# Windowed attention and a gated feed-forward block: scores of six groups in 64-key blocks on quarters of the matmul array

## The chip, the core and the metric

The kernel runs on one core of a Trainium2 chip. A core has a matmul engine (TensorE; PE for its matmuls and PEld for its weight loads in the profile), a vector engine (VectorE, DVE), a scalar engine (ScalarE, ACT), GpSimd (POOL) and SyncE (SP), which here only issues DMAs. Matmuls read SBUF and write PSUM, which has 8 banks; a bank holds 512 fp32 columns on each of 128 partitions. The metric is the time of one execution on the device in microseconds (us). The matmul array has 128 x 128 cells and can be divided into tiles; the profile writes a tile's rows and columns as 64\*128 or 64\*64.

## The reference

```python
scores = scale * np.matmul(q, k.transpose(0, 1, 3, 2))
is_sink = pos[None, :] < n_sink                 # 4
rel = pos[:, None] - pos[None, :]
in_window = (rel >= 0) & (rel < window)         # 128
scores = np.where(is_sink | in_window, scores, -1e9)
a = np.exp(scores - max); a = a / sum(a)
x = np.matmul(a, v)                             # tokens x (heads * 64)
g = x @ w_gate
out = (g * sigmoid(g) * (x @ w_val)) @ w_out
```

There are 4 batches, 8 heads, 768 positions and 64 elements a head; the feed-forward block has 3072 tokens, width 512 and inner width 1536. A query sees itself, the 127 keys before it and the first four keys of its batch.

## The kernel before, in words

The order of all instructions is written by hand. Attention runs in 12 groups of 256 queries, three to a batch (`b, c = divmod(g, 3)`); the feed-forward block runs in eight token blocks of 256 or 512. The two are interleaved on the same engines: `weave` goes through the feed-forward units (`gate`: gate and value projections of 128 inner columns, L414; `down`: output projection of 128 tokens, L499) and puts attention steps between their matmuls, at the units that `slots` and `pair` list (L686 to L719). Each engine runs its own instructions strictly in that order. Work for DVE that belongs to a step is put in the list `later` and issued at the next `flush`.

For a group, `step_S` (L271) makes the scores, transposed (keys on partitions, queries along the columns), for two pairs of heads at a time. The two heads of a pair lie on the upper and the lower 64 partitions of `kTs` and `qTs` and run as two row tiles of 64 x 128. Per head there are 512 columns: four blocks of 128 keys by 128 queries. For the query tile `j` (0 or 1) of 128 queries these are the keys of the tile before it (columns 256j) and its own keys (columns 256j + 128). ScalarE takes the exponential (L293) into `e`, and DVE multiplies two heads by a 0/1 mask (L298). About half of each block is masked away, since the window is a diagonal band. `step_K` (L302) makes the scores of the four sink keys for c > 0, and `step_sinks` (L322) multiplies them by the sink values. It opens four PSUM banks, one for each query tile and half of the heads, with one matmul each. `step_PV` (L332) then adds, for a query tile and four heads, two matmuls a head: `e` of the key tile before and of the own key tile, each times the values with a column of ones (65 columns, L349). The sum of exponentials comes out in column 65; DVE divides (L357, L363), and `step_X` (L369) turns the result for the feed-forward block, by a DMA transpose on SP's queue for all but the first three groups.

`step_sinks` is called at the start of the first `step_PV` of a group (query tile 0, heads 0 to 3). `PVs(g)` lists the four value steps with the head half as the outer loop, so the first two read heads 0 to 3.

Inputs come through GpSimd's DMA queue: `load_nat` (L104; four DMAs for a group's keys and queries), `load_v` (L116; two DMAs, 128 positions each, into a tile `va` of its own per group, whose ones DVE writes). Keys and queries of groups 4 to 11 are turned by `xbar` (L247) on SP's queue, and `load_nat` of the next group waits for that, since it has one buffer. `behind` and `turned` (L530 to L538) make GpSimd wait for a transposed tile, so that later loads don't start sooner.

The first groups have their own steps: group 0 `pair_T`, `pair_S` (L569 to L602), group 1 `step_T` (L214), where four transposes by matmul write every fourth column of a bank from quarters of 64 x 64. `pair_T` writes every second column (L575) from tiles of 128 x 64.

Of the kernel before, what the change touches and what calls it, by code (L numbers as in the profile page):

```python
# [7 lines left out]
FP32 = mybir.dt.float32  # L8
BF16 = mybir.dt.bfloat16
AF = mybir.ActivationFunctionType  # L10
ALU = mybir.AluOpType
# [3 lines left out]
def kernel(  # L15
# [12 lines left out]
    nc = tc.nc  # L28
    P = 128
    B, H, S, D = q.shape  # L30
# [9 lines left out]
    GC = S // 256  # L40
    NG = B * GC
    SIZES = [256, 256, 256, 512, 512, 512, 512, 256]
    assert sum(SIZES) == NTOK and NG == 12
    OFF = [sum(SIZES[:i]) for i in range(len(SIZES))]
    PEX = (0, 1, 2)

    VS = 72
    FCH = [2] * 6
# [2 lines left out]
    scale = 1.0 / float(D) ** 0.5  # L51
# [7 lines left out]
    const = pool("const", 1)  # L59
# [3 lines left out]
    vpool = pool("vpool", 1)  # L63
    kqtp = pool("kqtp", 2)
    epool = pool("epool", 2)
# [12 lines left out]
    def bank(shape, dtype, name):  # L78
        return psum.tile(shape, dtype, tag="b", name=name)
# [24 lines left out]
    def load_nat(g):  # L104
# [8 lines left out]
                    src[b, :, t0:t0 + P].rearrange("h p d -> p h d"))  # L113
        nats[g] = x

    def load_v(g):  # L116
        b, c = divmod(g, GC)
        va = vpool.tile([P, 2, H, VS], BF16, tag=f"va{g}", name="va")
        nc.vector.memset(va[:, :, :, D:D + 1], 1.0)
        for j in range(2):  # L120
            t0 = c * 256 + j * P
            nc.gpsimd.dma_start(  # L122
                va[:, j, :, 0:D], v[b, :, t0:t0 + P].rearrange("h p d -> p h d"))
        vas[g] = va
# [19 lines left out]
    ident = const.tile([P, P], BF16)  # L144
    mask = const.tile([P, 2, 256], BF16)
    mask0 = const.tile([P, 2, 256], BF16)
    diag_h = const.tile([P, 4], BF16)
    vcf = const.tile([P, 1, D + 1], FP32)
    vcl = const.tile([P, B - 1, D + 1], FP32)
# [28 lines left out]
    def load_sinks(t, b0, b1):  # L178
        for h in range(H):
            r = 32 * (h // 4) + NS * (h % 4)  # L180
            nc.sync.dma_start(
                t[r:r + NS, :, 0:D], v[b0:b1, h, 0:NS].rearrange("b s d -> s b d"))
# [18 lines left out]
    kTs, qTs, es_t, e_t, xns, xTs = {}, {}, {}, {}, {}, {}  # L201
    later = []
# [66 lines left out]
        vsbs.append(vsb)  # L269

    def step_S(g, p2, pps=(0, 1)):  # L271
        b, c = divmod(g, GC)
        if g not in e_t:
            e_t[g] = epool.tile([P, H, 512], BF16, tag="e", name="e")
        q0 = c * 256
        parts = [(q0, q0, 256, P), (q0 + P, q0 + P, P, 3 * P)]
        if c > 0:
            parts.insert(0, (q0 - P, q0, P, 0))
        lo = 0 if c > 0 else P
        pss = {2 * pp + h: bank([P, 512], FP32, "s") for pp in pps for h in range(2)}  # L280
        for pp in pps:
            p = 2 * p2 + pp
            for kk, qq, n, col in parts:
                for h in range(2):
                    r = slice(h * D, (h + 1) * D)
                    nc.tensor.matmul(  # L286
                        pss[2 * pp + h][:, col:col + n], kTs[b][r, p, kk:kk + P],
                        qTs[b][r, p, qq:qq + n], start=True, stop=True)
        m = (mask if c > 0 else mask0).rearrange("q (o a) x -> q o (a x)", o=1)
        for pp in pps:  # L290
            h0 = 4 * p2 + 2 * pp
            for h in range(2):
                nc.scalar.activation(  # L293
                    e_t[g][:, h0 + h, lo:512], pss[2 * pp + h][:, lo:512],
                    AF.Exp, scale=scale)

            def dve(e=e_t[g][:, h0:h0 + 2, lo:512]):
                nc.vector.tensor_tensor(  # L298
                    e, e, m[:, :, lo:512].broadcast_to([P, 2, 512 - lo]), op=ALU.mult)
            later.append(dve)  # L300

    def step_K(g):  # L302
# [17 lines left out]
    pos = {}  # L320

    def step_sinks(g):  # L322

        b, c = divmod(g, GC)
        for j in range(2):
            for hh in range(2):
                r = slice(32 * (2 * j + hh), 32 * (2 * j + hh + 1))
                pos[j, hh] = bank([P, 4, D + 1], FP32, "o")
                nc.tensor.matmul(pos[j, hh], es_t[g][r], vsbs[b][r], start=True,  # L329
                                 stop=False, skip_group_check=True)  # L330

    def step_PV(g, j, hh, norm="v"):  # L332
        b, c = divmod(g, GC)
        t = 2 * c + j
        if hh == 0:
            xns[g, j] = xnp.tile([P, DM], BF16, tag="xn", name="xn")
        if c > 0 and j == hh == 0:
            step_sinks(g)
        po = pos.pop((j, hh)) if c > 0 else bank([P, 4, D + 1], FP32, "o")
        mms = []  # L340
        for hq in range(4):
            h = 4 * hh + hq
            if t > 0:
                vp = vas[g][:, 0, h, 0:D + 1] if j else vas[g - 1][:, 1, h, 0:D + 1]
                mms.append((po[:, hq], e_t[g][:, h, 256 * j:256 * j + P], vp))
            mms.append((po[:, hq], e_t[g][:, h, 256 * j + P:256 * (j + 1)],
                        vas[g][:, j, h, 0:D + 1]))
        for i, (o, l, r) in enumerate(mms):
            nc.tensor.matmul(o, l, r, start=(c == 0 and i == 0),  # L349
                             stop=(i == len(mms) - 1),  # L350
                             skip_group_check=True)
# [21 lines left out]
    def step_X(g, j, evict="v"):  # L373
# [6 lines left out]
        elif tb > 1 and off == 0:  # L380
            xTs[tb] = dense(xtp.tile([P, DMC * 512], BF16, tag="xT", name="xT"),
                            DMC, SIZES[tb])
            if tb == 3:
                for i in range(2):
                    xTs[tb, i] = xTs[tb][:, :, 256 * i:256 * (i + 1)]
        if g not in PEX:
            def sp():
# [254 lines left out]
    nc.gpsimd.memset(vcl, 0.0)  # L642
    nc.gpsimd.memset(vcl[:, :, D:D + 1], 1.0)
    load_sinks(vcl, 1, B)

    step_T(1, 0, 0, "a")
    step_T(1, 0, 1, "a")
# [107 lines left out]
```

## Time and profile before

| | us |
|---|---|
| median of 3 runs | 238.09 |
| lowest and highest | 237.35, 238.37 |
| the profiled execution | 238.22 |
| its span, first to last instruction | 236.4 |
| PE busy | 228.7 |
| DVE, ACT, POOL busy | 157.5, 113.0, 75.3 |

In the profile a line such as `L349 PE MATMUL o<-va,e 128*128 128x65 bf16 x352 | 17.2, 194 | 0.1` gives the line of the kernel, the engine, the output and the inputs, the tile of the array, the shape of the moving operand, how many there were, the time in which at least one of them ran, the mean duration of one in ns, and the idle time of the engine in front of them. Matmuls overlap in time, so a mean duration of 194 ns does not say how often one starts. Lines that begin with a time are from the order in time: the start, the time covered by the merged group, the engine and the operation; consecutive instructions of one kind are merged into one line, and a few matmul records are missing from a trace. L numbers are lines of the kernel before.

### The profile page before, as it was taken

What the parts mean: (1) busy time and instruction counts of PE and PEld (TensorE: products, weight loads), DVE (VectorE), ACT (ScalarE), POOL (GpSimd) and SP (SyncE); (2) the same over time, 40 slices, a digit from 0 to 9 for tenths busy, and PEclk for the clock granted to TensorE, in tenths of its full rate; (3) what the DMA queues carried; (4) which work ended last, traced back from release to release, by engine and by line L of the source; (5) the groups of instructions that cost most, each with busy time, mean ns of one, the idle gap of its engine ahead of it and who ended that gap; (6) DMA issues with size and microseconds to landing.
All of it is one profiled execution on the core that took longest, in us unless ns stands there. A gap on an engine that the chain in (4) does not pass through costs nothing.

```text
span 236.4 us, 4873 instructions
## 1 busy us (share of the span) xinstructions
PE 228.7 (97%) x1867; PEld 127.7 (54%) x1893; DVE 157.5 (67%) x333; ACT 113.0 (48%) x230; POOL 75.3 (32%) x102
## 2 busy tenths in 40 slices
PE   8979999999999999999999999999999999999994
PEld 5659645795555644544445444444444445488443
DVE  4898888768650988960888980698970598877000
ACT  4784485467453836412836522655622663333221
POOL 8996875723501409204435350080000000000000
PEclk9999999999999999999999999999999999999999
DMA  7999999995998949997979996599314100200132
GB/s 137 156 191 176 182 199 205 159 145 79 153 225 168 134 72 76 129 134 172 144 114 136 132 140 168 133 87 116 67 24 143 58 3 0 44 3 1 47 132 90
DMA packets 108743, 27.62 MB, mean 117 GB/s; under 512 B 95792, under 2 KB 105776, under 8 KB 108720
## 3 DMA queue, kind: packets, MB, share of 16 engines
q0 software_dynamic: 76640, 13.90, 79.2%
q1 hardware_dynamic: 30672, 11.58, 25.2%
q10 hardware_dynamic: 1408, 1.84, 2.8%
q8 instruction: 15, 0.25, 0.4%
q14 instruction: 8, 0.07, 0.1%
HBM read 28.34 MB, written 6.29 MB: 147 GB/s over the span
## 4 chain that ended last, share of the span: by engine, by line
PE 89%; POOL 3%; DMA 3%; issue 1%; ACT 1%; DVE 1%; POOLq 0%; DVEq 0%; ACTq 0%
PE pv L414 26%; PE pd L499 26%; PE pg L414 26%; PE o L349 4%; PE s L286 4%; DMA wg<-in_moe_w_gate_dram 3%; POOL va L122 1%; POOL rows L100 1%; PE o L329 1%; PE pn L239 1%; POOL x L186 1%; ACT th L434 1%; PE pk L314 1%; PE px L393 0%; DVE u L442 0%
## 5 line engine op out<-in xcount | busy, mean ns | idle before, releaser
L442 DVE SCALAR_TENSOR_TENSOR u<-th,pg 128x512 bf16<-128x512 f32 x72 | 49.2, 683 | 39.4 <-ACT th L434 39.4
L414 PE MATMUL pg<-xT,wg 128*128 128x512 bf16 (+1 forms) x353 | 73.4, 336 | 1.9 <-DMA wg<-in_moe_w_gate_dram 1.2
L434 ACT ACTIVATE th<-pg 128x512 f32<-128x512 f32 x72 | 43.4, 603 | 63.1 <-PE pg L414 57.2
L414 PE MATMUL pv<-xT,wv 128*128 128x512 bf16 (+1 forms) x349 | 72.9, 336 | 0.6 <-ACT e L293 0.2
L499 PE MATMUL pd<-wo,ht 128*128 128x512 bf16 (+2 forms) x292 | 64.5, 371 | 0.5 <-issue 0.2
L414 PEld LDWEIGHTS <-wg 128*128 128x128 bf16 x360 | 35.0, 98 | 29.1 <-DMA wg<-in_moe_w_gate_dram 1.5
L453 DVE TENSOR_TENSOR ht<-u,pv 128x512 bf16<-128x512 bf16 x62 | 42.7, 688 | 9.4 <-PE pv L414 2.5
L293 ACT ACTIVATE e<-s 128x512 bf16<-128x512 f32 (+1 forms) x88 | 42.9, 583 | 3.7 <-PE s L286 3.6
L499 PEld LDWEIGHTS <-ht 128*128 128x128 bf16 x300 | 27.9, 98 | 30.3 <-issue 0.3
L414 PEld LDWEIGHTS <-wv 128*128 128x128 bf16 x360 | 32.1, 98 | 20.3 <-issue 1.7
L504 ACT ACTIVATE ot<-pd 128x512 f32<-128x512 f32 (+1 forms) x24 | 14.3, 596 | 46.7 <-PE pd L499 42.7
L111 POOL DMA_DIRECT2D nat<-in_k_dram x20 | 17.7, 890 | 39.5 <-DMA qT<-nat 35.8
L298 DVE TENSOR_TENSOR e<-e,mask 128x1024 bf16<-128x1024 bf16 (+1 forms) x44 | 27.1, 654 | 3.7 <-ACT e L293 3.7
L122 POOL DMA_DIRECT2D va<-in_v_dram x24 | 21.4, 917 | 4.7 <-DMA wo<-in_moe_w_out_dram 2.5
L363 DVE TENSOR_TENSOR xn<-o,rcp 128x256 bf16<-128x256 f32 x45 | 19.1, 424 | 1.5
L349 PEld LDWEIGHTS <-e 128*128 128x128 bf16 x352 | 15.2, 98 | 7.9 <-issue 0.2
L111 POOL DMA_DIRECT2D nat<-in_q_dram x20 | 17.7, 900 | 1.1 <-DMA wg<-in_moe_w_gate_dram 0.5
L349 PE MATMUL o<-va,e 128*128 128x65 bf16 x352 | 17.2, 194 | 0.1
L286 PE MATMUL s<-qT,kT 64*128 64x128 bf16 (+1 forms) x240 | 13.1, 238 | 0.0
L286 PEld LDWEIGHTS <-kT 64*128 64x128 bf16 x240 | 7.7, 94 | 7.4 <-issue 6.4
L506 DVE TENSOR_SCALAR ot<-pd 128x128 f32<-128x128 f32 x1 | 0.3, 292 | 14.3 <-PE pd L499 14.3
L357 DVE RECIPROCAL rcp<-o 128x4 f32<-128x4 f32 x48 | 8.3, 175 | 1.4 <-PE o L349 1.3
(74 smaller groups left out, 91.5 us busy)
## 6 DMA issues: line engine op xcount, KB each, us to landing
out_dram<-ot SPq DMA_DIRECT2D x17, 256.0 KB
va<-in_v_dram POOLq DMA_DIRECT2D x24, 128.0 KB, 6.2
nat<-in_k_dram POOLq DMA_DIRECT2D x20, 128.0 KB, 4.1
nat<-in_q_dram POOLq DMA_DIRECT2D x20, 128.0 KB, 5.5
wg<-in_moe_w_gate_dram POOLq DMA_DIRECT2D x6, 256.0 KB, 7.9
wv<-in_moe_w_val_dram POOLq DMA_DIRECT2D x6, 256.0 KB, 8.2
wo<-in_moe_w_out_dram POOLq DMA_DIRECT2D x4, 384.0 KB, 11.1
out_dram<-ot ACTq DMA_DIRECT2D x6, 256.0 KB
```

The source lines that it names most:

```text
L111: nc.gpsimd.dma_start(x[:, i, j].rearrange("p (h d) -> p h d", d=D), src[b, :, t0:t0 + P].rearrange("h p d -> p h d"))
L122: nc.gpsimd.dma_start(va[:, j, :, 0:D], v[b, :, t0:t0 + P].rearrange("h p d -> p h d"))
L286: nc.tensor.matmul(pss[2 * pp + h][:, col:col + n], kTs[b][r, p, kk:kk + P], qTs[b][r, p, qq:qq + n], start=True, stop=True)
L293: nc.scalar.activation(e_t[g][:, h0 + h, lo:512], pss[2 * pp + h][:, lo:512], AF.Exp, scale=scale)
L298: nc.vector.tensor_tensor(e, e, m[:, :, lo:512].broadcast_to([P, 2, 512 - lo]), op=ALU.mult)
L349: nc.tensor.matmul(o, l, r, start=(c == 0 and i == 0), stop=(i == len(mms) - 1), skip_group_check=True)
L363: nc.vector.tensor_tensor(xn, po[:, :, 0:D], rcp.broadcast_to([P, 4, D]), op=ALU.mult)
L414: nc.tensor.matmul(ps[:, i * n:(i + 1) * n], ws[fi][:, c, fo * P:(fo + 1) * P], xTs[tb][:, c], start=(c == 0), stop=(c == DMC - 1))
L434: nc.scalar.activation(th, pg, AF.Tanh, scale=0.5)
L442: nc.vector.scalar_tensor_tensor(u, th, 1.0, pg, op0=ALU.add, op1=ALU.mult)
L453: nc.vector.tensor_tensor(hts[tb][:, f:f + 512 // SIZES[tb]].rearrange("p a n -> p (a n)"), u, pv, op=ALU.mult)
L499: nc.tensor.matmul(po, hts[tb][:, f, ts * P:(ts + 1) * P], wos[f // n][:, f % n, lo:hi], start=(f == 0), stop=(f == DFC - 1))
```

## The change

The six groups `QG` = 4, 5, 7, 8, 10 and 11 (the second and third of batches 1 to 3) are computed in blocks of 64 keys.

- Scores (`step_Sq`): per head 384 columns instead of 512. The four 64-key blocks of the band go to quarters of the array: the head picks the upper or lower rows, the key block the lower or upper half of the columns. A pair of heads takes three runs of four matmuls (192, 128 and 64 columns). The exponential and the mask work on 384 columns. The mask `maskq` is built once on GpSimd, behind the loads of the first four groups, from pieces of `mask`.
- Values: the batch's values lie in a tile `vm` of six blocks of 128 positions that are shifted by 64 against the query tiles (`load_vm`: four DMAs for c = 1, two for c = 2, of which two bring 64 positions only; ones by GpSimd). `step_PV` has one matmul a head: the 128 keys from 64 before the query tile's start to 64 after it. What is left of the band are, per query tile and head, two corners of 64 keys by 64 queries. `step_sinks` does these on two diagonal quarters of the array, two at a time, for all eight heads and both query tiles: 32 matmuls of 65 columns, ahead of the first dense one.

PE has 480 instructions more (3788 and 4268 in all); GpSimd has 14 more, six of them DMAs.

```diff
+    QG = [g for g in range(4, NG) if g % GC]
...
+    def load_vm(g):
+        b, c = divmod(g, GC)
+        if b not in vms:
+            vms[b] = vpool.tile([P, 6, H, VS], BF16, tag=f"vm{b}", name="vm")
+            nc.gpsimd.memset(vms[b][:, :, :, D:D + 1], 1.0)
+        def part(t, hs, p0, p1, t0):
+            nc.gpsimd.dma_start(
+                vms[b][p0:p1, t - 1, hs, 0:D],
+                v[b, hs, t0:t0 + p1 - p0].rearrange("h p d -> p h d"))
+        for t in ((1, 2, 3, 4), (5, 6))[c - 1]:
+            p0, p1 = 64 * (t == 1), P - 64 * (t == 6)
+            part(t, slice(0, H), p0, p1, P * t - 64 + p0)
+
     def load_v(g):
+        if g in QG:
+            return load_vm(g)
...
     def step_S(g, p2, pps=(0, 1)):
+        if g in QG:
+            return step_Sq(g, p2, pps)
...
+    def step_Sq(g, p2, pps=(0, 1)):
...
+        q0 = c * 256
+        runs = (((q0, q0, 192, 0), (q0 + 64, q0 + 64, 192, 192)),
+                ((q0 + 128, q0 + 128, 128, 256), (q0 - 64, q0, 128, 0)),
+                ((q0 - 128, q0, 64, 192), (q0 + 192, q0 + 192, 64, 128)))
+        pss = {2 * pp + h: bank([P, 384], FP32, "s") for pp in pps for h in range(2)}
+        for pp in pps:
+            p = 2 * p2 + pp
+            for run in runs:
+                for odd, (kk, qq, n, col) in enumerate(run):
+                    part = slice(64 * (1 ^ odd), 64 * ((1 ^ odd) + 1))
+                    for h in range(2):
+                        r = slice(h * D, (h + 1) * D)
+                        nc.tensor.matmul(
+                            pss[2 * pp + h][part, col:col + n], kTs[b][r, p, kk:kk + 64],
+                            qTs[b][r, p, qq:qq + n], start=True, stop=True,
+                            skip_group_check=True)
...
     def step_sinks(g):
...
+        if g not in QG:
+            return
+        for j in range(2):
+            col, t = (192, 128)[j], 2 * c + j
+            for hq in range(4):
+                for hb in range(2):
+                    for odd in range(2):
+                        h = 4 * hb + hq
+                        r = slice(64 * (1 ^ odd), 64 * ((1 ^ odd) + 1))
+                        nc.tensor.matmul(
+                            pos[j, hb][64 * odd:64 * (odd + 1), hq],
+                            e_t[g][r, h, col:col + 64],
+                            vms[b][r, t + (0 if odd else -2), h, 0:D + 1],
+                            start=False, stop=False, skip_group_check=True)
...
     def step_PV(g, j, hh, norm="v"):
...
+            if g in QG:
+                mms.append((po[:, hq], e_t[g][:, h, 256 * j:256 * j + P],
+                            vms[b][:, t - 1, h, 0:D + 1]))
+                continue
...
     load_sinks(vcl, 1, B)
+    build_maskq()
```

More of the change, by code (lines that the diff above doesn't have):

```diff
@@ L114, in load_nat @@
         nats[g] = x
+    vms = {}
+    def load_vm(g):
[10 more added lines that the diff above has]
+            part(t, slice(0, H), p0, p1, P * t - 64 + p0)
     def load_v(g):
+        if g in QG:
+            return load_vm(g)
         b, c = divmod(g, GC)
@@ L146 @@
     mask0 = const.tile([P, 2, 256], BF16)
+    maskq = const.tile([P, 6, 64], BF16)
     diag_h = const.tile([P, 4], BF16)
@@ L300, in step_S, with build_maskq, dve @@
             later.append(dve)
+    def build_maskq():
+        nc.gpsimd.memset(maskq, 1.0)
+        if True:
+            for odd in range(2):
+                r = slice(64 * (1 ^ odd), 64 * ((1 ^ odd) + 1))
+                for m, sl in ((0, (1, 6, 4) if odd else (2, 4, 1)),
+                              (1, (2, 4, 1) if odd else (0, 5, 4))):
+                    x0_ = P * m + 64 * (1 ^ odd)
+                    o = maskq[r, sl[0]:sl[1]:sl[2]]
+                    nc.gpsimd.tensor_copy(
+                        out=o, in_=mask[r, 0:1, x0_:x0_ + 64].broadcast_to([64, 2, 64]))
+    def step_Sq(g, p2, pps=(0, 1)):
+        b, c = divmod(g, GC)
+        if g not in e_t:
+            e_t[g] = epool.tile([P, H, 512], BF16, tag="e", name="e")
+        q0 = c * 256
[14 more added lines that the diff above has]
+                            skip_group_check=True)
+        m = maskq.rearrange("q (o a) x -> q o (a x)", o=1)
+        for pp in pps:
+            h0 = 4 * p2 + 2 * pp
+            for h in range(2):
+                nc.scalar.activation(
+                    e_t[g][:, h0 + h, 0:384], pss[2 * pp + h], AF.Exp, scale=scale)
+            def dve(e=e_t[g][:, h0:h0 + 2, 0:384]):
+                nc.vector.tensor_tensor(
+                    e, e, m.broadcast_to([P, 2, 384]), op=ALU.mult)
+            later.append(dve)
     def step_K(g):
@@ L330, in step_sinks @@
                                  stop=False, skip_group_check=True)
+        if g not in QG:
[4 more added lines that the diff above has]
+                for hb in range(2):
+                    for odd in range(2):
+                        h = 4 * hb + hq
+                        r = slice(64 * (1 ^ odd), 64 * ((1 ^ odd) + 1))
+                        nc.tensor.matmul(
[3 more added lines that the diff above has]
+                            start=False, stop=False, skip_group_check=True)
     def step_PV(g, j, hh, norm="v"):
```

## The prediction

> **What bounds the kernel now.** I read the page's table of engines and its slices first, then the groups, then the order in time around the attention steps.
>
> ```profile
> span 236.4 us, 4873 instructions
> PE 228.7 (97%) x1867; PEld 127.7 (54%) x1893; DVE 157.5 (67%) x333; ACT 113.0 (48%) x230; POOL 75.3 (32%) x102
> PE   8979999999999999999999999999999999999994
> PE 89%; POOL 3%; DMA 3%; issue 1%; ACT 1%; DVE 1%; POOLq 0%; DVEq 0%; ACTq 0%
> L349 PE MATMUL o<-va,e 128*128 128x65 bf16 x352 | 17.2, 194 | 0.1
> ```
>
> The matmul engine is busy from end to end at the full granted clock, is 89% of the chain that ended last, and has waited 0.1 us ahead of 352 value matmuls. So a change counts by the length of PE's queue, and relief of the other engines counts nothing. What has to be priced is PE time from start to start; a record's own duration (194 ns) contains latency that overlaps. In order of time, group 7 on PE:
>
> ```profile
> 110.81 1.03 PE L414 MATMUL pg<-xT,wg 128*128 128x512 bf16 x4
> 111.77 0.62 PE L286 MATMUL s<-qT,kT 64*128 64x128 bf16 x12
> 112.31 0.29 PE L314 MATMUL pk<-qT,kss 128*32 128x128 bf16 x8
> 112.54 1.04 PE L414 MATMUL pv<-xT,wv 128*128 128x512 bf16 x4
> ...
> 120.20 0.29 PE L329 MATMUL o<-vsb,es 32*128 32x260 bf16 x4
> 120.43 0.42 PE L349 MATMUL o<-va,e 128*128 128x65 bf16 x8
> 120.68 1.03 PE L414 MATMUL pv<-xT,wv 128*128 128x512 bf16 x4
> ```
>
> Four 512-column matmuls from 110.81 take 4 x 0.216 = 0.865, to 111.67; scores start at 111.77: a change of the array's division costs about 0.1 us (the same 0.09 to 0.10 stands before L314, after it, and before and after L329). Scores of two head pairs end at 112.22, 0.442 us of streaming or 221 ns a pair: two heads run side by side, 512 columns at 0.417 ns = 213. Eight value matmuls take 0.25 us at most (120.43 to 120.68); their single starts lie 29.5 ns apart on average, 65 columns being 27.
>
> How quickly quarters go is the question, and three rows bear on it:
>
> ```profile
> L224 PE MATMUL pt<-ident,rows 64*64 64x64 bf16 x64 | 2.2, 244 | 0.0
> L575 PE MATMUL pt<-ident,x 128*64 128x128 bf16 x32 | 3.0, 389 | 0.3 <-DMA x<-in_q_dram 0.3
> L314 PE MATMUL pk<-qT,kss 128*32 128x128 bf16 x64 | 2.4, 225 | 0.0
> ```
>
> Their starts in narrow windows: L224 runs two diagonal quarters 3 ns apart, and a new two every 56 ns for 64 columns. L575 runs two column halves, a new two every 109 ns for 128 columns. L314 runs four column strips 3 ns apart; the second four start 67 ns after the first, 13 of it the first weight load, so 54 for 128 columns. The first two rows go at half rate, the third at full rate. What sets them apart is the output: L224 and L575 write every fourth or second column of their bank, L314 writes neighbours, as all the new matmuls do. The load of 64 weight columns costs 27 to 29 ns (L224's first two loads start at 10.542 and 10.571) and hides under a stream of that length.
>
> **The change, part by part.** Six groups (4, 5, 7, 8, 10, 11).
> - Scores: per pair 12 quarter matmuls replace 6; four run at once, in runs of 192, 128 and 64 columns: 83 + 56 + 30 = 169 ns against 221, taken as 170. Below: 163 (384 columns streaming). Above: 336, three runs in which two quarters and then two more go at L224's 56. I take 170, because L314 shows four tiles of one bank, their loads too, side by side. Per group 4 x -0.051 = -0.204 us (-0.23 to +0.46).
> - Dense values: 16 matmuls instead of 32: -16 x 29.5 ns = -0.472 us a group.
> - Quarters of the values: 32 matmuls, 16 twos. From 29 ns (stream and load both hidden) to L224's 56; I take 31, nearest to the contiguous row: +0.496 us a group (0.46 to 0.90). So the halved columns are paid back in full.
> - One more division of the array between sinks and dense values: +0.098 us.
> - Sum: -0.204 - 0.472 + 0.496 + 0.098 = -0.082 a group, x 6 = -0.5 us.
>
> The Trainium skill's page "PSUM — Partial Sum Buffer", Specifications, gives PSUM 8-byte lines and says that non-contiguous outputs slow matmuls; this agrees with L224 and L575 against L314 and would leave the quarters at about 30 ns. The Trainium skill's page "TensorEngine Tiling (Array Packing)", Gotcha 1, speaks against the change: different row tiles cannot use one PSUM bank at the same time, and each two value quarters do that. By this rule a two would take two streams one after the other, 54 ns and more, and the sum would be some +2.0 us instead of -0.5. L224's two row tiles share a bank as well, and its 56 ns is what the half rate alone makes, so the row shows no such turn-taking on top.
>
> **A new wait.** The quarters sit in the sink step, in front of the first dense values, and read all eight heads, where the first value step read heads 0 to 3. So the masks of heads 4 to 7 are due earlier, and PE runs in order: behind the waiting quarter stand the values and all projections. In group 4 the second scores come just ahead:
>
> ```profile
> 64.77 0.62 PE L286 MATMUL s<-qT,kT 64*128 64x128 bf16 x12
> 65.32 1.04 PE L499 MATMUL pd<-wo,ht 128*128 128x512 bf16 x4
> 66.29 0.31 PE L329 MATMUL o<-vsb,es 32*128 32x260 bf16 x4
> 66.54 0.42 PE L349 MATMUL o<-va,e 128*128 128x65 bf16 x8
> ...
> 66.32 0.69 DVE L298 TENSOR_TENSOR e<-e,mask 128x1024 bf16<-128x1024 bf16 x1 [1.49 <-ACT e L293]
> 67.30 0.69 DVE L298 TENSOR_TENSOR e<-e,mask 128x1024 bf16<-128x1024 bf16 x1 [0.29 <-ACT e L293]
> ```
>
> Masks end at 67.01 and 67.99; sinks begin at 66.29. With the change exponentials start at 65.17 and, of 384 columns, span 1.64 us as in the first groups (89.19 to 90.83); masks take 0.55 (the 768-element form of L298): heads 4 and 5 ready at 66.68, heads 6 and 7 at 67.45. PE would start quarters at 66.40. It waits 0.25 us for head 4 (second two) and 0.65 for head 6 (sixth two): +0.9 us once (0 if the exponentials overlap better, up to 1.2). In groups 5, 7 and 11 the masks end 0.6 us ahead of the sinks (83.71 to 84.30; 119.61 to 120.20; 192.43 to 193.02). In groups 8 and 10 they end 0.13 after them, but shorter masks come 0.2 to 0.3 earlier and head 6 is read 0.3 after the sinks: nothing.
>
> **What is hidden.** ACT loses 48 x (613 - 502) = 5.3 us and DVE 24 x (691 - 553) = 3.3: off the path. GpSimd gains the mask (one memset, four copies; 64-partition copies there take 0.19 to 0.39, so 1.7 us) ahead of group 4's k and q loads; they stand at 41.90 and 43.78 with 0.23 and 1.01 us of idle, so they come 0.4 late, and their transposes, issued by SP from 49.81 to 55.03, leave 6 us until scores at 61.06. The ones column is set by GpSimd three times (about 0.1 each) and no longer by DVE six times (0.07). Each of groups 4, 7, 10 gets two more value issues, 2 x 0.92 us, just before GpSimd idles 7.4, 12.5 and 14.6 us for transposes. Values land 10.1 us after issue at worst: group 4's at about 62.6, needed at 66.4; the others have more. SP's own issues do not change in number or order. If this cover failed, a late load would cost PE its lateness one for one.
>
> Total: -0.5 + 0.9 = +0.4: 238.22 + 0.4 = 238.6. The profiled execution's 238.22 is its span plus 1.8 us around it, and 0.13 above the median 238.09.
>
> **Rivals.**
> - B, quarters at L224's half rate whatever the output. A value two is 56 and the short runs of scores are 56 as well: 83 + 56 + 56 = 195 a pair. Per group -0.10 - 0.47 + 0.90 + 0.10 = +0.42, x 6 = 2.5, and a wait of 0.75 in group 4: 241.5, slower. For it: the only 64 x 64 row of the trace. Against: L575, at half rate with whole rows, and L314. It decides from 39 ns a two on, where the sum passes +1.2 us.
> - C, four quarters of scores don't run together: 336 a pair, +0.46 a group; with quarters at 31 to 56, 242.6 to 244.8. L314 speaks against it.
> - E, the wait in group 4 delays its transposed outputs (transfer waited for until 75.17), then group 6's loads (75.94) and its transposes (done 88.19), only 0.6 us ahead of its scores (88.82). If contention takes that margin and 1.4 us more: about 240.1.
> - D, faster: no wait in group 4 and a value two at 29: -0.8 makes 237.4, still within 0.5%; faster needs 1.2 us, so hidden waits that the shorter exponentials remove. PE's 0.1 us ahead of L349 speaks against it: about 236.9.
>
> **How the numbers follow.** Forecast A (238.6; own range 237.4 to 239.4): 0.52. B 0.27, C 0.08, E 0.07, D 0.06. This kernel can be told from no change from about 0.5% (1.2 us) on. Faster is D, 0.06; same is A, 0.52; slower is B, C and E, 0.42. The range, 237.2 to 242.0, holds A, B and E and leaves out C and most of D.
>
> **What would show it.** Value quarters: a new two every 29 to 31 ns (A) or 56 (B). Scores: 0.34 us for 12 + 12 matmuls (A), 0.39 (B), 0.67 (C). Group 4: an idle stretch of some 0.9 us in front of quarters, put down to DVE's masks. No idle PE at 61 or 88. Wrong would be: quarters that take turns, or waits in more groups than the fourth.

## The result and the profile after

The changed kernel takes 238.48 us (median of 6 runs, 238.42 to 238.95); the kernel before takes 237.59 (6 runs, 237.33 to 238.37). The ratio is 1.0043, 95% interval 1.0031 to 1.0054: slower by less than the 0.5% that the prediction set as its bound, with an interval that does not hold 1. (The ratios in this document are those on record; they can differ a little from the quotient of two medians, which is 1.0037 here.) The forecast time was 238.6, but the forecast difference was +0.4 us against a profiled execution of 238.22, which turned out to lie 0.6 above the median; the measured difference is +0.9. The profiled execution of after took 238.53, with a span of 236.8.

Page after: the span, the engines, the slices of PE and of its clock, and the chain by engine.

```profile
span 236.8 us, 5392 instructions
...
PE 230.5 (97%) x2133; PEld 128.7 (54%) x2133; DVE 154.2 (65%) x327; ACT 108.5 (46%) x230; POOL 80.9 (34%) x116
...
PE   8899999999999999999999999999999999999994
...
PEclk9999999999999999999999999999999999999999
...
PE 88%; POOL 3%; DMA 3%; DVE 2%; ACT 2%; issue 1%; POOLq 0%; DVEq 0%; ACTq 0%
```

PE is still the bound from end to end, and at the full clock. ACT has become 4.5 us shorter and DVE 3.3 (5.3 and 3.3 were forecast), which buys nothing. POOL has gained 5.6 us. DVE now has 2% of the chain where it had 1%.

The groups of after that the change brought (instruction count, busy time, mean ns of one, idle time in front and what ended it). From here on L numbers are lines of the kernel whose trace is shown:

```profile
L436 PE MATMUL o<-va,e 128*128 128x65 bf16 x160 | 7.7, 194 | 0.0
L436 PE MATMUL o<-vm,e 128*128 128x65 bf16 x96 | 6.6, 194 | 0.0
L355 PE MATMUL s<-qT,kT 64*64 64x64 bf16 (+2 forms) x288 | 6.5, 221 | 0.0
L409 PE MATMUL o<-vm,e 64*64 64x65 bf16 x192 | 4.5, 193 | 0.5 <-DVE e L367 0.5
```

L436 is the dense value matmul, half as many in the six groups; L355 the scores on quarters; L409 the values on quarters. Only L409 has a wait of note: 0.5 us, for DVE's mask. In order of time, PE in group 7:

```profile
112.12 0.53 PE L355 MATMUL s<-qT,kT 64*64 64x192 bf16 x24
112.58 0.30 PE L383 MATMUL pk<-qT,kss 128*32 128x128 bf16 x8
...
120.39 0.29 PE L398 MATMUL o<-vsb,es 32*128 32x260 bf16 x4
120.61 0.69 PE L409 MATMUL o<-vm,e 64*64 64x65 bf16 x32
121.23 0.30 PE L436 MATMUL o<-vm,e 128*128 128x65 bf16 x4
121.37 1.02 PE L501 MATMUL pv<-xT,wv 128*128 128x512 bf16 x4
```

From scores to L383 are 0.46 us (0.54 before). From sinks to the projection behind the first value step are 0.98 us (0.48 before), since 32 quarters stand in between. In the single records a new two of quarters starts every 31.8 ns. The three other value steps of the group save 0.122 us each. So PE's queue per group is: scores 2 x -0.083, values +0.50 - 0.37, together -0.03 us.

Group 4 in order of time, PE and DVE's masks:

```profile
64.02 0.53 PE L355 MATMUL s<-qT,kT 64*64 64x192 bf16 x24
...
65.33 0.56 DVE L367 TENSOR_TENSOR e<-e,maskq 128x768 bf16<-128x768 bf16 x1 [1.75 <-ACT e L363]
65.45 0.29 PE L398 MATMUL o<-vsb,es 32*128 32x260 bf16 x4
65.67 0.59 PE L409 MATMUL o<-vm,e 64*64 64x65 bf16 x10
66.10 0.56 DVE L367 TENSOR_TENSOR e<-e,maskq 128x768 bf16<-128x768 bf16 x1 [0.21 <-ACT e L363]
66.71 0.53 PE L409 MATMUL o<-vm,e 64*64 64x65 bf16 x22 [0.45 <-DVE e L367]
```

The first mask ends at 65.89 and the second at 66.66; the second two of the quarters starts 0.24 us late and the sixth another 0.62 late (gaps between starts, less the usual distance), 0.86 us in all. Ten quarters take 0.59 here, where 32 take 0.69 in group 7.

To add this up, I compare when PE reaches the same step in both traces, counted from the first gate projection (start-up before it differs between executions by more than the effect: 16.1 us before, 15.3 after). At the scores of group 4, after is 0.1 us behind; between the second scores of group 4 and the scores of group 5 it falls back by 0.90; over all the rest by another 0.25. At the end it is 1.18 us behind. In the two profiled executions the longer start-up of before hides most of this (238.53 against 238.22 us); the medians, over executions with other start-ups, differ by 0.9.

The 0.25 stand where the five groups behind group 4 should have gained 0.03 each. Three places make them: PE falls back by 0.24 at the first scores of group 6, by some 0.09 at those of group 8 and by 0.08 at those of group 10. Group 6 keeps the old form. In order of time, its scores and the projection behind them, before and after:

```profile
88.82 0.50 PE L286 MATMUL s<-qT,kT 64*128 64x256 bf16 x8
89.42 1.04 PE L414 MATMUL pv<-xT,wv 128*128 128x512 bf16 x4
```

```profile
89.05 0.62 PE L309 MATMUL s<-qT,kT 64*128 64x256 bf16 x8
89.90 0.39 PE L501 MATMUL pv<-xT,wv 128*128 128x512 bf16 x1 [0.23 <-DVE xn L450]
```

In both, the projection starts 0.06 us after DVE has normalised the last value step of group 5 (`xn`, done at 89.36 and 89.84), so here DVE sets the pace. PE's value steps have become shorter, and PE waits 0.23 us instead of 0.10. At group 8, PE waits 0.19 us for `xn` in the same way, ahead of the scores of the sink keys; before it had no such wait, but one of 0.18 just behind. The 0.08 at group 10 I did not trace to a cause.

### The profile page after: what moved, and what is told of

It is laid out like the page before. It is cut to its first block, busy times and chain, and to the rows that moved or that the text cites. A ratio compares the mean times of both kernels' runs of the same rounds, so it can differ in the third digit from the quotient of the medians.

```text
span 236.8 us, 5392 instructions
## 1 busy us (share of the span) xinstructions
PE 230.5 (97%) x2133; PEld 128.7 (54%) x2133; DVE 154.2 (65%) x327; ACT 108.5 (46%) x230; POOL 80.9 (34%) x116
## 4 chain that ended last, share of the span: by engine, by line
PE 88%; POOL 3%; DMA 3%; DVE 2%; ACT 2%; issue 1%; POOLq 0%; DVEq 0%; ACTq 0%
PE pv L501 26%; PE pd L586 26%; PE pg L501 26%; PE o L436 3%; DMA wg<-in_moe_w_gate_dram 3%; PE s L355 2%; PE o L409 2%; POOL va L142 1%; PE s L309 1%; POOL rows L101 1%; PE pn L260 1%; PE pk L383 1%; POOL x L207 1%; ACT e L363 1%; PE o L398 1%
## 5 line engine op out<-in xcount | busy, mean ns | idle before, releaser
L501 PE MATMUL pv<-xT,wv 128*128 128x512 bf16 (+1 forms) x360 | 74.2, 337 | 0.3 <-DVE xn L450 0.2
L501 PE MATMUL pg<-xT,wg 128*128 128x512 bf16 (+1 forms) x360 | 74.1, 336 | 0.4 <-DMA wg<-in_moe_w_gate_dram 0.3
L501 PEld LDWEIGHTS <-wg 128*128 128x128 bf16 x360 | 35.1, 98 | 28.1 <-DMA wg<-in_moe_w_gate_dram 0.5
L501 PEld LDWEIGHTS <-wv 128*128 128x128 bf16 x360 | 32.0, 98 | 19.9 <-issue 0.8
L363 ACT ACTIVATE e<-s 128x384 bf16<-128x384 f32 x48 | 19.6, 504 | 3.7 <-DMA out_dram<-ot 2.4
L316 ACT ACTIVATE e<-s 128x384 bf16<-128x384 f32 (+1 forms) x40 | 18.1, 552 | 0.3 <-PE s L309 0.2
L436 PEld LDWEIGHTS <-e 128*128 128x128 bf16 x256 | 12.3, 98 | 7.4 <-issue 0.2
L127 POOL DMA_DIRECT2D vm<-in_v_dram x18 | 14.9, 864 | 0.4 <-DMA nat<-in_q_dram 0.4
L367 DVE TENSOR_TENSOR e<-e,maskq 128x768 bf16<-128x768 bf16 x24 | 12.4, 551 | 3.2 <-ACT e L363 3.2
L142 POOL DMA_DIRECT2D va<-in_v_dram x12 | 10.7, 914 | 5.1 <-DMA wo<-in_moe_w_out_dram 2.5
L321 DVE TENSOR_TENSOR e<-e,mask 128x768 bf16<-128x768 bf16 (+1 forms) x20 | 11.3, 604 | 0.4 <-ACT e L316 0.4
```

Of the source, the lines that this page charges most:

```text
L127: nc.gpsimd.dma_start(vms[b][p0:p1, t - 1, hs, 0:D], v[b, hs, t0:t0 + p1 - p0].rearrange("h p d -> p h d"))
L316: nc.scalar.activation(e_t[g][:, h0 + h, lo:512], pss[2 * pp + h][:, lo:512], AF.Exp, scale=scale)
L363: nc.scalar.activation(e_t[g][:, h0 + h, 0:384], pss[2 * pp + h], AF.Exp, scale=scale)
L436: nc.tensor.matmul(o, l, r, start=(c == 0 and i == 0), stop=(i == len(mms) - 1), skip_group_check=True)
L501: nc.tensor.matmul(ps[:, i * n:(i + 1) * n], ws[fi][:, c, fo * P:(fo + 1) * P], xTs[tb][:, c], start=(c == 0), stop=(c == DMC - 1))
```

## Experiments

Two theories of the loss stood at first. The first (theory W in the expectations): PE's own queue is about neutral and the wait in group 4 is the loss. The rival (rival L): the loss is spread over all six groups (quarters, divisions or hidden waits), and group 4 is no special case. Each ratio below is against the kernel before on the same chip; "PE falls back" is the comparison of order in time just described, in the profiled execution.

**early4: group 4's second scores earlier, so that its masks are done in time.**

```diff
-        (4, TN(2)[::2]), (5, TN(2)[1::2]), ((6, 7), Ss(2)), (6, [K(2)]),
+        (20, Ss(4)[1:]), (4, TN(2)[::2]), (5, TN(2)[1::2]), ((6, 7), Ss(2)), (6, [K(2)]),
...
-        (19, [L(Ss(4)[0], K(4))]), (20, Ss(4)[1:]),
+        (19, [L(Ss(4)[0], K(4))]),
```

> Edit: the changed kernel, with the second scores of group 4 put first instead of last among the attention steps of their unit (8 output projections, 1.7 us, earlier). Theory W (the six groups' queue on PE is as long as before, and the loss is the one wait in group 4, 0.85 us in the profile): no idle PE among the value quarters, and 0.85 us less than the changed kernel: the time of the kernel before, within 0.2 us. Rival L (the queue is longer in every group, and a wait in group 4 only takes up slack that would have come later): the changed kernel's time, +0.9 us against the kernel before.

237.85 us, ratio 1.0028 (1.0004 to 1.0052). Order in time of early4, the masks and PE in group 4:

```profile
65.37 0.56 DVE L367 TENSOR_TENSOR e<-e,maskq 128x768 bf16<-128x768 bf16 x1 [0.21 <-ACT e L363]
...
65.61 0.29 PE L398 MATMUL o<-vsb,es 32*128 32x260 bf16 x4
...
65.83 0.69 PE L409 MATMUL o<-vm,e 64*64 64x65 bf16 x32
```

The wait is gone: all 32 quarters take 0.69. PE falls back by 0.19 us in all, instead of 1.18. The ratio says less than the trace: its interval overlaps that of after. Single executions lie from 237.4 to 240.0; eight of twelve are below 238.0, with a median 0.2 above before, where none of after's six is below 238.4. So the wait is most of the loss: 0.99 of 1.18 us in the traces, and some 0.5 of 0.9 between the medians. Something else makes the other four executions long.

**without4: group 4 keeps the old form.**

```diff
-    QG = [g for g in range(4, NG) if g % GC]
+    QG = [g for g in range(5, NG) if g % GC]
...
-        for t in ((1, 2, 3, 4), (5, 6))[c - 1]:
+        for t in ((1, 2, 3, 4), (5, 6) if g > 5 else (3, 4, 5, 6))[c - 1]:
```

> Edit: the changed kernel with group 4 left in the old form, so five groups instead of six; the values of group 5 then come with four DMAs of their own. Theory W: the wait goes and five groups of about -0.02 us remain: -0.3 to +0.1 us against the kernel before. Rival L: five sixths of the loss remain, +0.7 us.

238.11 us, ratio 1.0024 (1.0004 to 1.0044); PE falls back by 0.26. As in early4 the big loss goes with the wait in the trace. The time, 0.6 above before, is not what the first theory expected (-0.3 to +0.1) and lies nearer to the rival's +0.7; the trace shows 0.26, and no loss shared by all five groups, which speaks against the rival.

**early4_mask: early4, and the mask built while GpSimd is idle** (early4's edit stands as well).

```diff
     load_sinks(vcl, 1, B)
-    build_maskq()
...
-        (11, [NV(4), lambda: nc.gpsimd.tensor_copy(out=vcl[64:128], in_=vcl[0:64])]),
+        (11, [NV(4), lambda: nc.gpsimd.tensor_copy(out=vcl[64:128], in_=vcl[0:64]),
+              build_maskq]),
```

> Edit: the changed kernel with the second scores of group 4 early, and the mask built on GpSimd only after the values of group 4 are on their way, where GpSimd idles. Theory T: keys and queries of group 4 are issued 1.5 us earlier on GpSimd, the chain of transposes up to group 6 is earlier by 0.4 to 1 us, and the kernel is 0 to 0.3 us faster than with the early scores alone: 0 to +0.3 us against the kernel before. If the place of the mask does not matter: +0.35 us, as with the early scores alone.

(Theory T is the one that scores_va below tests: the added value loads delay the transposes, and with them later loads.)

237.96 us, ratio 1.0032 (1.001 to 1.0054); PE falls back by 0.18. The place of the mask changes nothing that PE sees. But the trace tells something that I had not looked for: GpSimd issues group 5's keys when group 4's transposes have landed, and this comes 1.5 us later than before, counted from the first gate projection (57.69 - 15.53 against 56.81 - 16.11), although group 4's own loads are now issued on time (25.82 and 25.79). What remains ahead of it is the added value loads of group 4. SP's transposes and GpSimd's next keys, in before and in after:

```profile
52.50 2.53 SPq L253 DMA_TRANSPOSE qT<-nat  x2
56.81 1.75 POOL L111 DMA_DIRECT2D nat<-in_k_dram  x2 [7.43 <-DMA qT<-nat]
```

```profile
52.13 2.52 SPq L274 DMA_TRANSPOSE qT<-nat  x2
58.00 1.75 POOL L112 DMA_DIRECT2D nat<-in_k_dram  x2 [7.92 <-DMA qT<-nat]
```

From the end of the last issue to the keys that wait for its landing pass 1.78 us in before, 3.34 in after and 2.91 in early4_mask; start-up plays no part in that. It is 1.78 to 1.82 us in all seven kernels of this record that load group 4's values with two DMAs (before, packed_T, scores_va, without4, twos4, fours4, fours4_late), and 2.75 to 3.34 in all seven that use four or five, wherever the mask is built.

**split: the quarters of heads 4 to 7 move in front of their own dense values**, at the price of more divisions of the array.

```diff
         if g in QG:
             corners(g, 0)
...
+        if g in QG and j == 0 and hh == 1:
+            corners(g, 1)
```

> Edit: the changed kernel, with the value quarters of heads 4 to 7 not in the sink step but ahead of the first dense values of these heads: the array's division changes twice more in each of the six groups, and nothing waits for the masks of heads 4 to 7 sooner than in the kernel before. Theory W: -0.85 us for the wait, + 6 x 0.22 us for two more changes of the division (0.095 each, and 0.02 of exposed first loads) = +0.5 us against the changed kernel, +1.35 against the kernel before. Rival L: +1.3 against the changed kernel, +2.2 against the kernel before.

238.91 us, ratio 1.0062 (1.0038 to 1.0085), +1.4 us: the first theory's number, but not a proof of its sum. The profiled execution (240.38, above the median; PE falls back by 1.8 us in it) shows a wait that belongs to neither theory. The waits of PE in split:

```profile
PE s L355 <- DMA qT<-nat: 0.8, 1, 0.8
```

It is at the scores of group 5, whose transposed queries come late. That is what the prediction's rival E described, one group earlier.

**scores_alone: quarter scores, and two dense value matmuls a head instead of one and the quarters.** It reads wrong positions of `vm`; the loads are those of after.

```diff
-        if g not in QG:
-            return
+        return
...
             if g in QG:
-                mms.append((po[:, hq], e_t[g][:, h, 256 * j:256 * j + P],
-                            vms[b][:, t - 1, h, 0:D + 1]))
+                for x in range(2):
+                    mms.append((po[:, hq], e_t[g][:, h, P * (j + x):P * (j + x + 1)],
+                                vms[b][:, t - 1, h, 0:D + 1]))
```

> Edit: scores in quarters as changed; the value quarters are left out and the dense values take two matmuls a head on the first 384 columns, as many and as long as in the kernel before (so the output is not the reference's). Both theories: 12 score steps, each 0.08 us shorter on PE from its start to the next group of matmuls (0.545 to 0.462 us in the profiles), no wait in group 4: -1.0 us against the kernel before. If the exponentials or masks set the pace in these stretches after all, more than -1.5; if the shorter scores are given back elsewhere, nothing.

237.44 us, ratio 0.999 (0.9965 to 1.0015), where -1.0 us was expected: a miss. The shorter scores are there: PE is 0.28 ahead by group 5's second scores. Then it stops. Order in time on PE in scores_alone (an execution of 238.79, above the median):

```profile
89.34 0.51 PE L309 MATMUL s<-qT,kT 64*128 64x256 bf16 x8 [1.09 <-DMA qT<-nat]
...
148.76 1.04 PE L501 MATMUL pg<-xT,wg 128*128 128x512 bf16 x4 [0.78 <-DMA xT<-xn]
```

The first is the scores of group 6, for transposed queries; the second the gate projection of block 5, for the transposed outputs of groups 7 and 8. Neither wait is in the trace of before or of after. PE came earlier and found the transposes late. Single executions go from 236.4 to 238.8, and one took 240.6.

**scores_va: the same scores, with the values loaded as before (two DMAs a group), and the mask built late.** Against scores_alone it has six value loads fewer, and no mask build ahead of group 4's loads; early4_mask shows that the mask's place does not matter for PE.

```diff
     def load_v(g):
-        if g in QG:
-            return load_vm(g)
...
             if g in QG:
-                mms.append((po[:, hq], e_t[g][:, h, 256 * j:256 * j + P],
-                            vms[b][:, t - 1, h, 0:D + 1]))
+                for x in range(2):
+                    vp = vas[g][:, 0, h, 0:D + 1] if j else vas[g - 1][:, 1, h, 0:D + 1]
+                    mms.append((po[:, hq], e_t[g][:, h, P * (j + x):P * (j + x + 1)],
+                                vas[g][:, j, h, 0:D + 1] if x else vp))
```

> Edit: the scores in quarters alone, as before, but now the values are loaded as in the kernel before (no shifted tiles, two DMAs a group) and the mask is built on GpSimd only after the values of group 4 (again the dense values take the first 384 columns, so the output is not the reference's). Theory T (in the run with the scores alone, the 1.0 us that PE saved was given back as waits for transposed inputs at group 6 and for transposed outputs ahead of block 5, because the added loads made that chain of transfers 1.3 to 2 us later): without the added loads no wait of PE over 0.5 us at these two places, and -1.0 us against the kernel before. Rival S (PE merely catches up with a chain of transfers that is as late as in the kernel before): the waits stay, 0 to -0.3 us.

236.49 us (236.19 to 236.85), ratio 0.9962 (0.9949 to 0.9974): -0.95 us as expected, with no wait on a transpose in the list of PE's waits. PE gains 1.02 us over six groups, 0.17 a group; the prediction said 0.204. Group 5's keys are issued 0.5 us later than before, counted from the first gate projection, instead of 1.3 in scores_alone. So the saving on PE does reach the end where the value loads are few; this speaks for the added loads as what eats it in scores_alone.

**values_alone: the old scores with the new values** (`step_S` never calls `step_Sq`; group 4's scores early as in early4).

```diff
-        if g in QG:
-            return step_Sq(g, p2, pps)
```

> Edit: scores of 512 columns, exponentials and masks as in the kernel before; values as changed (loads, value quarters, one dense matmul a head; they read the first 384 columns, so the output is not the reference's); second scores of group 4 early, so that nothing waits there. Theory W: per group, 16 twos of 0.032, one more change of the division with its first load of 0.12 to 0.14, less 16 matmuls of 0.0295: +0.17 us, x 6 = +1.0 us against the kernel before. If the value quarters took L224's 0.056 a two: +0.55 a group, +3.3 us.

239.49 us, ratio 1.0083 (1.0068 to 1.0099): +2.0 us, between the two numbers expected. Its waits explain most of the excess. PE waits for DVE's `xn` at groups 6 and 8 (0.24 and 0.18 us) and 0.2 us at block 5 for transposed outputs. Above all, group 4 waits again; its old exponentials and masks are the longer ones.

```profile
66.97 0.53 PE L407 MATMUL o<-vm,e 64*64 64x65 bf16 x22 [0.57 <-DVE e L319]
```

0.73 us from start to start are that wait. In groups 10 and 11 PE falls back by 0.14 and 0.13 a group, as the value steps of after say (+0.50 - 0.37). A value two at 56 ns would make 0.5 a group; that is excluded.

**packed_T: the kernel before, with the 64 x 64 transposes of group 1 writing neighbouring columns** instead of every fourth; ACT and DVE put them in order when they copy.

```diff
-                        pt[h, pp, r:256:4], x[h, i, p, r * D:(r + 1) * D],
+                        pt[h, pp, 64 * r:64 * (r + 1)], x[h, i, p, r * D:(r + 1) * D],
```

> Edit: the kernel before; the transposes of group 1 (64 x 64 quarters, two at a time, 64 columns) write 64 neighbouring columns of their bank instead of every fourth, and the copies out of PSUM put them in order. If the output's step sets their rate: a new two every 30 ns instead of 56. If it is the shape (64 x 64, two row tiles in one bank): still 56 ns. The time is no test, since what follows waits for weights: 237.5 us, within 0.5.

237.49 us, ratio 1.0013 (0.9999 to 1.0027). The group of these 64 matmuls, in packed_T:

```profile
L224 PE MATMUL pt<-ident,rows 64*64 64x64 bf16 x64 | 1.6, 194 | 0.6 <-DMA rows<-in_q_dram 0.6
```

Before, the prediction shows it with 2.2 us and 244 ns. A new two starts every 31.7 ns instead of every 56. The step of the output alone set the lower rate, and rival B falls by its own row.

**twos4: the change in groups 7, 8, 10 and 11 only, mask late.**

```diff
-    QG = [g for g in range(4, NG) if g % GC]
+    QG = [g for g in range(6, NG) if g % GC]
```

> Edit: the change as it is, two quarters at a time, but in groups 7, 8, 10 and 11 alone (none of which waits for masks), mask built where GpSimd idles. Theory W: four groups of -0.02 to 0: 0 us, within 0.3, against the kernel before. Rival L: four sixths of the change's loss, +0.6 us.

238.70 us, ratio 1.0063 (1.0041 to 1.0085), although group 4 is not in it. The profiled execution (241.25, the longest of twelve) waits 1.7 us at block 5 for transposed outputs; its row `PE pg L501 <- DMA xT<-xn: 1.7, 1, 1.7` has the same times as that of the next kernel. (Another 1.5 us of this one execution are lost before group 2, where the granted clock was 0.57 from 16 to 20 us.) The median is 1.3 above before: the first theory's 0 is wrong here, and so is the rival's +0.6. So the wait in group 4 is most of the loss of after, but not the only loss that this change can have: the theory needed a second half.

**fours4: twos4 with the corners of both query tiles on four quarters at once.** The corners of tile 0 stay on the anti-diagonal quarters; those of tile 1 go to the diagonal ones, for which a second tile `vx` brings 2 x 64 positions (two loads more a group, one fewer of `vm`), and the scores write these blocks to other halves (a fourth run, 28 matmuls instead of 24 a step).

```diff
-                        r = slice(64 * (1 ^ odd), 64 * ((1 ^ odd) + 1))
+                for j, r, o, vv in ((0, hi, lo, vms[b][hi, t - 2, h, 0:D + 1]),
+                                    (0, lo, hi, vms[b][lo, t, h, 0:D + 1]),
+                                    (1, lo, lo, vxs[g][lo, h, 0:D + 1]),
+                                    (1, hi, hi, vxs[g][hi, h, 0:D + 1])):
```

> Edit: the change in groups 7, 8, 10 and 11 alone, with the value quarters of both query tiles at once: the corners of the second query tile are made in the other half of the partitions (one more 64-column run of two score matmuls a pair), and the values for them come in a small tile of 2 x 64 positions a group in its place (two more DMAs a group); so four quarters of the array work at a time, 8 fours instead of 16 twos; the mask is built where GpSimd idles. Theory W: per group scores -0.17, values +0.17 - 8 x 0.032 = -0.08, together -0.25 or a little less for the extra run; x 4 = -0.9 us against the kernel before. If the extra loads or the extra run eat it: 0.

238.09 us, ratio 1.0028 (1.0 to 1.0055), where -0.9 us was expected: a miss in time, not on PE. Order in time of group 10 in fours4:

```profile
170.28 0.29 PE L405 MATMUL o<-vsb,es 32*128 32x260 bf16 x4
...
170.88 0.42 PE L444 MATMUL o<-vm,e 128*128 128x65 bf16 x8
```

Sinks to the first dense value are 0.60 us, against 0.84 in after (120.39 to 121.23): four quarters, their loads too, run side by side. PE is 0.26 ahead after the scores of groups 7 and 8. Then, in PE's waits in fours4:

```profile
PE pg L509 <- DMA xT<-xn: 1.7, 1, 1.7
```

**fours6: the same in all six groups, group 4's scores early.**

```diff
-    QG = [g for g in range(6, NG) if g % GC]
+    QG = [g for g in range(4, NG) if g % GC]
...
-        (19, [L(Ss(4)[0], K(4))]), (20, Ss(4)[1:]),
+        (19, [L(Ss(4)[0], K(4))]),
```

> Edit: as the run with four quarters at a time, in all six groups, with the second scores of group 4 early. Theory W: 6 x -0.25 = -1.4 us on PE; theory T adds that the loads of groups 4 and 5 (three more DMAs for group 4, two more for group 5) make the chain of transposes later, so that part comes back as waits of PE at the scores of group 5 or 6: between -1.4 and -0.3 us against the kernel before.

238.37 us, ratio 1.0043 (1.002 to 1.0065). The profiled execution (237.94) now waits at block 3, where group 4's outputs are turned:

```profile
74.85 1.03 PE L509 MATMUL pg<-xT,wg 128*128 128x256 bf16 x8 [0.87 <-DMA xT<-xn]
```

Over groups 7 to 11 PE then gains 0.9 us. The first half of the expectation (PE's saving) holds; the wait came at another place than the scores of group 5 or 6, and the time, +1.0, is outside what was expected.

**fours4_late: fours4, with one group's value loads moved.** By now the question was whether the value loads cause these waits or only lie beside them. `NV(10)` issues `load_nat` and `load_v` of group 10. In fours4 its value loads (L133, L127) are issued while SP issues the transposes of block 5's outputs (L483). Order in time of fours4, SP's queue and GpSimd:

```profile
138.91 1.42 POOL L133 DMA_DIRECT2D vx<-in_v_dram  x2
140.26 2.51 POOL L127 DMA_DIRECT2D vm<-in_v_dram  x3
```

```profile
138.46 1.19 SPq L483 DMA_TRANSPOSE xT<-xn  x1
140.36 2.26 SPq L483 DMA_TRANSPOSE xT<-xn  x1
```

```diff
-        (3, [NV(10)]), (15, [A(xbar, 10)]), (15, [NV(11)])))
+        (3, [A(load_nat, 10)]), (15, [A(xbar, 10)]),
+        (15, [A(behind, 5, 511), A(load_v, 10), NV(11)])))
```

> The kernel of fours4 (groups 7, 8, 10, 11; the corners of both query tiles on four quarters of the array at once; mask built late), with one edit: the value loads of group 10 are issued some 10 us later, behind the landing of the transposed outputs for block 5, instead of together with group 10's q and k loads. Two theories of the 1.9 us that PE waited in fours4 for those transposed outputs. Theory L (the added value loads lie on the DMA queues when the outputs are transposed and lengthen that transfer): the wait at the begin of block 5 falls to under 0.4 us, what PE's shorter queue saves (0.7 to 0.9 us over four groups) stays, and the time is 236.4 to 236.9, ratio 0.996 to 0.998. Theory C (the transposes are late for what stands before them on SP's queue or on the cores' own engines, and group 10's loads only happen to lie there): the wait of 1.5 to 2 us stays and the time is 237.8 to 238.3, ratio 1.002 to 1.004. Theory M (the loads only move the collision): no wait at block 5 but one of 0.5 us or more at the scores of group 10 or 11 or at the begin of block 6, and 237.2 to 237.8.

236.55 us (236.47 to 236.82), ratio 0.9961 (0.9948 to 0.9975): faster than both kernels, within the first theory's numbers (Theory L of that expectation; the letters there are its own). Order in time on PE at block 5, first fours4, then fours4_late:

```profile
148.73 1.04 PE L509 MATMUL pg<-xT,wg 128*128 128x512 bf16 x4 [1.73 <-DMA xT<-xn]
```

```profile
146.64 1.03 PE L509 MATMUL pg<-xT,wg 128*128 128x512 bf16 x4
```

SP's and GpSimd's queues in fours4_late:

```profile
141.40 1.23 SPq L483 DMA_TRANSPOSE xT<-xn  x1
```

```profile
144.73 0.17 POOL L627 CAST warmed<-xT 1x1 f32<-1x1 bf16 x1 [6.08 <-DMA xT<-xn]
...
145.24 1.38 POOL L133 DMA_DIRECT2D vx<-in_v_dram  x2
```

L627 is `behind`, which waits for the transposed tile. The last transpose is issued at 141.40 and has landed by 144.73, within 3.3 us. In fours4 it is issued between 140.36 and 142.62, and PE was released only at 148.73: at least 6.1 us. Nothing but the place of group 10's value loads, and the wait that holds them there, differs. No wait on a transpose is left in the list of PE's waits, PE keeps the 0.9 us that it saves over four groups, and the five executions lie within 0.35 us of each other. Those of fours4 spread over 3.1, or over 1.7 without the longest, whose granted clock was 0.993.

## Why the prediction was right, and where it was not

- **PE is the bound; relief of ACT and DVE counts nothing.** Right: 97% of the span, 88% of the chain.
- **Dense values, -0.472 a group; quarters at 31 ns a two; +0.098 for a division.** Right: -0.122 a step is -0.49, a two takes 31.8, and quarters with their division come to +0.62 (0.594 forecast). The contiguous L314 rather than the 64 x 64 L224 was the right row, for the reason given: packed_T shows L224's low rate to come from the step of its output. Rivals B and C have nothing left. (The 109 ns that the prediction reads for L575 hold in the later part of that row; its first eight twos, from 4.15 to 5.56 us, start some 213 ns apart.)
- **The two rules.** The Trainium skill's page "PSUM — Partial Sum Buffer", Specifications, says that outputs that aren't contiguous slow matmuls; packed_T agrees, 56 against 31.7 ns. The page "TensorEngine Tiling (Array Packing)", Gotcha 1, has different row tiles not use one PSUM bank at the same time; each two value quarters do so here, at 31.8 ns a two, where taking turns was to make 54 or more. (At 54 the prediction's own terms add up to +1.7 us rather than its +2.0.) The measurement decides: on this kernel the rule costs no time.
- **Scores, 170 ns a pair.** Half right: the second pair takes 170, the first 191, because the first weight load behind a change of division shows with some 20 ns (107 ns from the first four matmuls to the second, 86 in the second pair), where in before it showed with 11 (66 and 55). Per step -0.083 instead of -0.102, which makes 0.23 us over twelve steps. With the quarters' small excess a group saves 0.03 instead of 0.082, the six groups 0.2 instead of 0.5 us.
- **Group 4 waits 0.9 us for the masks of heads 4 to 7.** Right in place, cause and size: 0.24 and 0.62 us against 0.25 and 0.65. early4 takes it away, and PE's loss falls from 1.18 to 0.19.
- **DVE behind the shorter value steps.** The prediction gave this no price. PE waits for `xn` at the scores of groups 6 and 8, as shown above. At group 6 the wait is 0.23 to 0.24 us in after, early4, without4, early4_mask, values_alone and fours6, whose group 5 has the new values, and 0.10 to 0.11 in before, packed_T, twos4, fours4, fours4_late and scores_va, whose group 5 has the old ones. (split does not show it, and scores_alone waits for a transpose there.) So at group 6 DVE, off the path on average, takes back what two value steps save.
- **Sum.** -0.2 + 0.86 is +0.7, and the three places behind group 4 add 0.4, which makes up PE's 1.18 to within 0.1. Forecast +0.4, measured +0.9. That 238.6 came so near 238.48 is in part luck: the base was 0.6 above the median and the difference 0.5 too small, and the two nearly cancel.
- **"They come 0.4 late", the cover of GpSimd's added work.** Group 4's own loads did about that: counted from the first gate projection its keys are issued 1.3 us later, the last of its four loads 0.1. What the cover missed comes behind them: group 5's keys are issued 2.0 us later, 1.3 in early4, and 1.5 in early4_mask with the mask out of the way. I counted GpSimd's instructions in its own queue, and the value loads' landing against its own deadline, and gave no price to what these loads do to transposes on the same DMA engines. In the trace of after nothing came of it; as forecast, there is no idle PE at the scores of groups 4 and 6.
- **Rival E (a transposed tile only just in time) at 0.07** is not what after shows, but its mechanism is real. It is not triggered by the wait in group 4, as I had it, but by value loads that lie on the DMA queues when a transpose runs. For fours4 moving the loads shows this; for scores_alone taking them out does (scores_va); twos4 and fours6 have waits of the same kind, for which nothing was moved.
- **Rival D (faster once the wait is gone).** early4, without the wait, is still at 1.0028; the quarters two at a time have next to nothing to give. With four at a time and the loads moved, 0.9961.

Still open: the 0.08 us at group 10, and why early4, without4 and early4_mask, whose profiled executions are only 0.2 to 0.3 us behind on PE, have medians 0.4 to 0.6 above before. That some executions meet a late transpose fits the spread of their times; no trace of theirs shows one. The granted clock is not it: in before, every execution above 238.5 has a clock of 0.993 or less, while those of early4 from 238.7 to 240.0 have 0.999 and more. A longer start-up is not excluded, since the only trace of before is one of its longer executions. That the late keys of group 5 come from the loads, as at block 5, rests on the fourteen traces compared above; moving these loads alone was not tried.

## What to carry to other kernels

Here, dividing the array into quarters paid only by how many run at once: two quarters at a time gave back what half the columns saved (0.51 against 0.49 us a group, and the change of division on top), four at a time saved 0.23 us a group, scores included. When a change adds DMA loads, do not only ask whether they land in time; look for the transposes that run on the DMA engines in those microseconds and for the margin that PE has behind them, since a saving on PE uses up that margin first. An engine that is off the path on average can still set the pace behind a step that has become shorter; look at what the next step waits for. If a kernel's single executions spread over some 2 us at full granted clock, while those of its neighbours stay within 0.4 to 0.7, such a collision may be the cause: in fours4 moving the loads ended the spread.

## What was not expected of the hardware

- A PSUM output that writes every fourth column made 64-column matmuls start every 56 ns a two instead of 31.7 (quarters of 64 x 64).
- Four quarters of 64 x 64 run at once, weight loads included, with two row tiles on each of two banks: 32 value matmuls and the change of division behind them in about 0.38 us (170.50 to 170.88) instead of 0.62.
- After a change of division the first load of 64 weight columns shows with some 20 ns: the second two of value quarters starts 53 ns after the first, later ones 29 to 36 ns apart.
- Five value loads of 64 or 128 KB, issued within 4 us around two DMA transposes, turned a landing within 3.3 us into one of at least 6.1 (fours4_late and fours4, one trace each).
